# A long convolution by two short Fourier steps: an inverse of 64x64 cosine and sine sums instead of 64x128 complex ones

## The chip, the cores and the metric

The kernel runs on one core of a Trainium2 chip. The metric is the device time of one execution in microseconds; several executions are timed and their median is given. One execution is also recorded by the hardware profiler.

## The reference, cut to what matters

Two results for 2048 positions of 512 channels are mixed by a gate that depends on the position:

```python
x = A_u                                              # (1, 2048, 512)
g = sigmoid((x * gate_w).sum(-1, keepdims=True))
# a: a convolution along the 2048 positions
P = exp((dt * A)[:, :, None] * l)                    # 512 x 128 x 2048
K = einsum("dn,dnl,dn->dl", C, P, dt * B).real       # 512 filters of 2048 taps
y = irfft(rfft(pad(u)) * rfft(pad(K)))[:2048]        # transforms over 4096
a = y + u * Dskip
# b: a dense part
b = gelu(x @ w1 + b1) @ w2 + b2                      # 512 -> 1792 -> 512
return g * a + (1 - g) * b
```

All of it is in float32.

## The kernel before, in words

The program has two stages. The **front** (up to about 427 us) computes the 512 filters, the dense part b and a first short Fourier step of signal and filters; its order on every engine is written out by a planner that gives each piece a cost and a due time. The planner and the front are the same in both kernels. The front leaves in DRAM two arrays, tu_d for the signal and tk_d for the filters, of 32 frequencies with 128 rows of 512 channels each (64 points, real and imaginary). It also leaves the dense part's share of the output, already multiplied by 1 - g, in the output array itself.

The second stage, `conv`, has a hand-written order. Its loop runs over s = 0 to 15, two frequencies n = 2s and 2s + 1 at a time, and everything in it is 512 channels wide:

- `fetch` (L1056, L1059) brings a frequency's filter rows into a tile tk, of which there are eight, and for every fourth frequency a tile cc of matrices; L1179 brings the signal rows that did not fit before the loop. All of these are issued by SP.
- `taps` (bank p2k) and `signal` (bank p2u) are the second Fourier step: per s four matmuls each, with 128 rows and 64 output columns, the two frequencies of s side by side (L1084). ACT copies p2k to k (L1092).
- `product` multiplies signal and filter as complex numbers on DVE: six operations (L1106 to L1111) that give v, real and imaginary, two frequencies on top of each other in 64 rows each.
- `inverse` (bank pa, L1123) takes a frequency's 64 points back: for each of the two frequencies two matmuls of 64 rows by 128 columns, one with the real part of v and the matrix from cc, one with the imaginary part and a matrix g that `matrices` builds from cc on ACT (L1070, L1071). The 128 columns are 64 points, real and imaginary in turn.
- `turn` copies pa into one of six slots sa (ACT, L1129) and stores it to t4_d in DRAM (SP, L1131, shown as t_d). After each eighth frequency the group is read back with rows and frequencies exchanged into t3 (L1138, shown as t): four loads of 512 KB, issued by POOL for the first three groups and by ACT for the last.
- From s = 6 to 13, `dense` (L1148) loads the dense part's output rows back, 512 KB at a time, on SP.

On PE the order within one s is: signal of s + 1, taps of s + 2, inverse of s. On SP it is: the loads for three s later, then the stores of s, then dense's load. SP issues in order, and the program gives its transfers eight semaphores in turn, so each waits for the landing of the one eight before.

After the loop PE does what is left of the dense part (`rest`, L1159 to L1161) and four matmuls whose result nobody reads (`warm`, L1197). Then follows the last stage, eight rounds m of 2 x 128 output rows: in each, eight matmuls of 64 rows by 32 columns combine the 32 frequencies (bank pb, L1208), and the result is multiplied by g and added to the dense part, on DVE alone (L1219) or on ACT and POOL (L1216, L1217). SP stores each round (L1223); the last round leaves in two stores, on SP and ACT (L1221).

Of the kernel before, what the change touches and what calls it, by code (L numbers as in the profile page):

```python
# [9 lines left out]
F32 = mybir.dt.float32  # L10
# [7 lines left out]
P = 128  # L18
L = 2048
D = 512  # L20
# [53 lines left out]
N_US = N_ATTIC + N_LOFT  # L74
W_DVE = ((1, 0), (3, 0), (5, 0))

GROUP = 8

ASIDE = (1, 3, 6, 8, 11, 13)
PI = float(np.pi)  # L80
TWO_PI = 2.0 * PI
TURN = 2.0**32
# [12 lines left out]
def k0_order():  # L95
    return [8 * (n % 4) + n // 4 for n in range(32)]


def seat(n):

    return 4 * (n % 8) + n // 8


def constants():
# [10 lines left out]
    qn = np.arange(64)  # L115
# [6 lines left out]
    rows = np.zeros((2, 64, 32))  # L122
    for n, k in enumerate(k0_order()):
        rows[:, seat(n)] = er.T[k] / L
        rows[:, seat(n) + 32] = ei.T[k] / L
    g1 = rows.reshape(P, 32)

    ko = k0_order()  # L130
    f2 = np.zeros((32, 2, 64, 64))
    g2 = np.zeros((32, 64, 64, 2))
    for n, k in enumerate(ko):
        er, ei = om(4 * (q[:, None] * k + 32 * np.outer(q, k1)) + q[:, None])
        f2[n, 0], f2[n, 1] = er, -ei
        er, ei = om(4 * (qn[None] * k + 32 * np.outer(k1, qn)) + qn[None])
        g2[n, :, :, 0], g2[n, :, :, 1] = er, -ei
    f2 = f2.reshape(8, 4, P, 64).transpose(0, 2, 1, 3).reshape(8, P, 256)
    g2 = g2.reshape(8, 2, P, P).transpose(0, 2, 1, 3).reshape(8, P, 256)
# [111 lines left out]
def gated_mix(  # L251
# [18 lines left out]
    nc = tc.nc  # L270
# [5 lines left out]
    t4_d = dr.tile([4, 2, 2, GROUP, 32, D], F32, name="t4_d")  # L276
# [766 lines left out]
    def conv(pool, ps, late, attic, loft):  # L1043
# [3 lines left out]
        zs = [pool.tile([P, D], F32, name=f"z{k}", bufs=1) for k in range(2)]  # L1047
        us = places(attic, loft)
        ko = k0_order()
        c4s, mats, t2s = {}, {}, {}  # L1050

        def fetch(n):
            if n % 4 == 0:
                m = n // 4
                cc = pool.tile([P, 2, 256], F32, tag="cc", name=f"cc{m}", bufs=4)
                nc.sync.dma_start(cc, c2[m].rearrange("p (a b) -> p a b", a=2))  # L1056
                c4s[m] = cc
            t2s[n] = pool.tile([P, D], F32, tag="tk", name=f"tk{n}", bufs=N_TK)
            nc.sync.dma_start(t2s[n], tk_d[ko[n]])  # L1059

        def matrices(m):

            cc = c4s[m]
            f = cc[:, 0].rearrange("p (n k) -> p n k", n=4)
# [5 lines left out]
            nc.scalar.mul(g1[:, :, :, 0], g[:, :, :, 1], -1.0)  # L1070
# [43 lines left out]
        def inverse(s):  # L1114

            v = prod.pop(s)
            for i in range(2):
                pas[2 * s + i] = ps.tile([P, D], F32, tag="pa", name=f"pa{s}{i}", bufs=2)
            for c in range(2):
                w = mats[s // 2][1][c][:, s % 2]  # L1120
                for i in range(2):
                    r = slice(64 * i, 64 * i + 64)
                    nc.tensor.matmul(pas[2 * s + i], w[r], v[c][r], start=(c == 0), stop=(c == 1))  # L1123

        def turn(s):

            for n in (2 * s, 2 * s + 1):
                sa = sas[n % 6]
                nc.scalar.copy(sa, pas.pop(n))  # L1129
                g, k = divmod(n, GROUP)  # L1130
                nc.sync.dma_start(t4_d[g, :, :, k].rearrange("i c q d -> q (i c) d"), sa)  # L1131
                if k < GROUP - 1:
                    continue
                rows = t4_d[g].rearrange("i c k q d -> (i c k) q d")

                for h in range(0, 32, 8):
                    on = nc.gpsimd if n < 31 else nc.scalar
                    on.dma_start(t3[g:P:4, h : h + 8], rows[:, h : h + 8])  # L1138
# [25 lines left out]
        for n in range(N_TK):  # L1164
            fetch(n)
            if n == 1:
                t3 = pool.tile([P, 32, D], F32, name="t3", bufs=1)
                g1t = pool.tile([P, 32], F32, name="g1t", bufs=1)
        nc.sync.dma_start(g1t, g1)
        matrices(0)  # L1170
        taps(0)
        signal(0)
# [21 lines left out]

        warm = ps.tile([P, D], F32, tag="pa", name="warm", bufs=2)
        for _ in range(N_KEEP):
            nc.tensor.matmul(warm[0:64], mats[7][0][1][:, 3], zs[0], start=True, stop=True)  # L1197
        for s in range(N_LATE):
            z = mos[7][:, s]
            nc.vector.scalar_tensor_tensor(z, accs[s], gate[:, 1, 14 + s : 15 + s], z, ALU.mult, ALU.add)  # L1200

        for m in range(8):
            tag, n = ("pa", 2) if m % 3 == 2 else ("pu", 4)
            pbs = [ps.tile([P, D], F32, tag=tag, name=f"pb{m}{i}", bufs=n) for i in range(2)]
            for b in range(4):
                for i in range(2):
                    r = slice(64 * i, 64 * i + 64)
                    nc.tensor.matmul(  # L1208
                        pbs[i][32 * b : 32 * b + 32], g1t[r], t3[r, 4 * m + b], start=True, stop=True
                    )  # L1210
            for i in range(2):
                t = 2 * m + i
                z, g = mos[m][:, i], gate[:, 0, t : t + 1]
                if t in ASIDE:
                    a = sas[ASIDE.index(t)]
                    nc.scalar.mul(a, pbs[i], g)  # L1216
                    nc.gpsimd.tensor_add(z, z, a)  # L1217
                else:
                    nc.vector.scalar_tensor_tensor(z, pbs[i], g, z, ALU.mult, ALU.add)  # L1219
                if m == 7:  # L1220
                    (nc.sync, nc.scalar)[i].dma_start(out[t], z)  # L1221
            if m < 7:
                nc.sync.dma_start(out[2 * m : 2 * m + 2].rearrange("s p d -> p s d"), mos[m])  # L1223
# [22 lines left out]
def layout(inputs):  # L1246
# [4 lines left out]

    xl = xpq[:, qs].reshape(32, 16, 4, D).transpose(1, 2, 0, 3).reshape(16, P, D)

    xs = xpq.reshape(32, 8, 4, 2, D).transpose(1, 3, 2, 0, 4).reshape(16, P, D)
# [47 lines left out]
```

## Time and profile before

| | us |
|---|---|
| median of 3 runs | 552.06 |
| lowest, highest | 548.29, 552.96 |
| the profiled execution | 547.97 |
| its span, first to last instruction | 546.1 |
| loop over s, first inverse to last | 436.5 to 517.9 |
| last stage, first pb to the end of the span | 529.2 to 546.1 |

The profile names engines (PE for matmuls, PEld for their weight loads, DVE, ACT, POOL, SP) and writes each group as line, engine, operation, output<-input. A q behind an engine's name is its queue, the part that issues transfers and waits. A float32 matmul of the kernel shows as two instructions. Busy times of matmuls that run side by side overlap, so the distance from start to start tells more than the time of one. The share of DMA is the mean over the core's 16 DMA engines; it can pass 1 a little, as packets that share an engine are counted one by one.

### The profile page before, as it was taken

To read this page: it belongs to the slowest core of one execution; us is meant where nothing else is said; L and a number is where in the kernel's file an instruction comes from. 1 tells how busy PE (TensorE), PEld (TensorE's weight loads), DVE (VectorE), ACT (ScalarE), POOL (GpSimd) and SP (SyncE) were. 2 spreads that over 40 slices of the span, in tenths; PEclk is the share of its full clock that TensorE was granted. 3 is DMA by queue.
4 is the path that set the end of the run, shared out by engine and by line. 5 is a ranking of instruction groups with operands and counts; after the bars stand their busy time and mean duration, and the time that the engine had idled before them with its cause. 6 is when DMAs were issued, how large, how long until landed. Compare 5 with 4: busy or idle time off the path is not lost.

```text
span 546.1 us, 12354 instructions
## 1 busy us (share of the span) xinstructions
PE 523.0 (96%) x4882; PEld 393.9 (72%) x4882; DVE 426.8 (78%) x806; ACT 371.4 (68%) x630; POOL 41.3 (8%) x79
## 2 busy tenths in 40 slices
PE   7869999999999999999999999999999899999993
PEld 6637788998898879787988889889889533333450
DVE  6798999999999949979998899999311567676523
ACT  4989847799956599968659986496263554555312
POOL 2000000000000000000101010110011001010104
PEclk9869999999999999999999999999999999999998
DMA  8998583153683352564984227525539979999958
GB/s 264 335 298 291 199 262 106 69 166 112 144 266 134 116 158 78 184 230 98 215 271 96 79 39 176 96 80 117 156 42 190 315 259 294 370 368 402 338 216 308
DMA packets 82469, 108.35 MB, mean 198 GB/s; under 512 B 39446, under 2 KB 42522, under 8 KB 81900
## 3 DMA queue, kind: packets, MB, share of 16 engines
q1 hardware_dynamic: 77020, 86.56, 49.6%
q0 software_dynamic: 5056, 18.65, 13.2%
q10 hardware_dynamic: 336, 2.36, 1.2%
q8 instruction: 38, 0.62, 0.5%
q14 instruction: 19, 0.16, 0.1%
HBM read 61.93 MB, written 45.62 MB: 197 GB/s over the span
## 4 chain that ended last, share of the span: by engine, by line
PE 72%; DMA 11%; issue 5%; ACT 5%; SPq 2%; DVE 2%; POOL 1%; POOLq 0%; ACTq 0%; DVEq 0%
PE pk L653 10%; PE acc L917 8%; PE acc L919 8%; PE ph L869 8%; PE acc L918 7%; PE ph L870 7%; PE ph L871 7%; PE p2u L1084 5%; PE p2k L1084 5%; PE pa L1123 4%; DMA tu_d<-attic 2%; PE ph L378 2%; DMA attic<-in_xs_dram 2%; SPq L693 1%; ACT sk L678 1%
## 5 line engine op out<-in xcount | busy, mean ns | idle before, releaser
L869 PE MATMUL ph<-xh,wh 128*128 128x256 f32 x448 | 129.1, 288 | 4.0 <-ACT attic L396 2.2
L871 PE MATMUL ph<-xh,wl 128*128 128x256 f32 x448 | 128.0, 286 | 0.5 <-DVE wl L752 0.4
L870 PE MATMUL ph<-xlo,wh 128*128 128x256 f32 x448 | 127.7, 285 | 0.0
L869 PEld LDWEIGHTS ph<-xh,wh 128*128 128x128 f32 x448 | 86.2, 192 | 13.9 <-issue 4.8
L870 PEld LDWEIGHTS ph<-xlo,wh 128*128 128x128 f32 x448 | 86.3, 193 | 1.9
L917 PE MATMUL acc<-wh,hh 128*128 128x512 f32 x210 | 85.3, 406 | 2.1 <-ACT hh L889 1.9
L871 PEld LDWEIGHTS ph<-xh,wl 128*128 128x128 f32 x448 | 86.3, 193 | 1.1 <-DVE wl L752 1.1
L919 PE MATMUL acc<-wh,hl 128*128 128x512 f32 x210 | 83.4, 397 | 0.2 <-DVE hl L899 0.2
L918 PE MATMUL acc<-wl,hh 128*128 128x512 f32 x210 | 83.0, 395 | 0.0
L886 ACT ACTIVATE ph<-ph,b1t 128x256 f32<-128x256 f32 x112 | 50.4, 450 | 40.5 <-PE ph L871 38.5
L899 DVE TENSOR_TENSOR hl<-ph,hh 128x512 fp32r<-128x512 f32 (+1 forms) x62 | 38.3, 618 | 34.8 <-ACT hh L889 34.7
L653 PE MATMUL pk<-y,xc 128*32 128x64 f32 x2048 | 61.4, 290 | 0.0
L653 PEld LDWEIGHTS pk<-y,xc 128*32 128x32 f32 x2048 | 57.2, 136 | 3.7 <-issue 1.4
L917 PEld LDWEIGHTS acc<-wh,hh 128*128 128x128 f32 x210 | 39.8, 190 | 17.9 <-issue 7.6
L919 PEld LDWEIGHTS acc<-wh,hl 128*128 128x128 f32 x210 | 39.8, 190 | 11.5 <-DVE hl L899 2.8
L615 DVE TENSOR_TENSOR y<-y,ea 128x64 f32<-128x64 f32 (+4 forms) x80 | 45.3, 566 | 0.2
L918 PEld LDWEIGHTS acc<-wl,hh 128*128 128x128 f32 x210 | 39.7, 189 | 6.7
L460 DVE TENSOR_TENSOR loft<-xc,zz 128x256 f32<-128x256 f32 (+2 forms) x48 | 37.2, 776 | 2.4 <-ACT xc L586 2.0
L889 ACT CAST hh<-ph 128x512 fp32r<-128x512 f32 (+1 forms) x62 | 33.0, 533 | 7.5 <-PE acc L918 4.1
L461 DVE TENSOR_TENSOR loft<-xc,zz 128x256 f32<-128x256 f32 (+2 forms) x48 | 37.2, 774 | 0.0
L628 DVE TENSOR_TENSOR y<-y,loft 128x2048 f32<-128x2048 f32 x16 | 36.5, 2284 | 0.0
L1092 ACT COPY k<-p2k 128x512 f32<-128x512 f32 x32 | 18.7, 585 | 22.2 <-issue 12.2
(172 smaller groups left out, 923.3 us busy)
## 6 DMA issues: line engine op xcount, KB each, us to landing
tu_d<-attic SPq DMA_DIRECT2D x64, 128.0 KB, 3.6
tk_d<-sk SPq DMA_DIRECT2D x32, 256.0 KB, 4.5
tk<-tk_d SPq DMA_DIRECT2D x32, 256.0 KB, 5.1
t_d<-sa SPq DMA_DIRECT2D x32, 256.0 KB, 5.2
t<-t_d POOLq DMA_DIRECT2D x12, 512.0 KB, 7.5
attic<-tu_d SPq DMA_DIRECT2D x22, 256.0 KB, 4.3
attic<-in_xt_dram SPq DMA_DIRECT2D x16, 256.0 KB, 4.1
xh_d<-xh SPq DMA_DIRECT2D x8, 512.0 KB, 3.9
```

What stands on the lines that cost most here:

```text
L460: vec(2 * m, lambda: vv.tensor_mul(t, a, br), due, [ka, *kb], [kt])
L615: nc.vector.tensor_mul(both(n, 64 - 3 * n, n), both(0, 64 - n, n), an)
L653: nc.tensor.matmul(pks[q][32 * j : 32 * j + 32, gg], x[:, r, :, ch], y[:, r, :, ch], start=(r == 0), stop=(r == 1), skip_group_check=True,)
L869: nc.tensor.matmul(p, h, xh[xk][:, d], start=(d == 0), stop=False)
L870: nc.tensor.matmul(p, h, xlo[xk][:, d], start=False, stop=False)
L871: nc.tensor.matmul(p, lo, xh[xk][:, d], start=False, stop=(d == 3))
L886: nc.scalar.activation(phs[q][:, n], phs[q][:, n], AF.Gelu_apprx_tanh, bias=b1t[:, f : f + 1])
L899: nc.vector.tensor_sub(lo, phs[q][:, 0:nf], hi.bitcast(F32))
L917: nc.tensor.matmul(a, h, wh[1][w], start=start, stop=False)
L918: nc.tensor.matmul(a, h, wl[1][w], start=False, stop=False)
L919: nc.tensor.matmul(a, l, wh[1][w], start=False, stop=(j == 3))
L1084: nc.tensor.matmul(out[64 * i : 64 * i + 64], w, x, start=True, stop=True)
```

## The change

The inverse is taken about the middle of its 64 points. Instead of complex rows, each frequency's inverse gives sums with cosines and with sines at 32 distances from the middle: two matrices of 64 rows by 32 columns, side by side in 64 columns, real and the same for the real and the imaginary part of v. The two parts are written to the upper and lower 64 rows of pa. So a frequency has two matmuls of 64 rows by 64 columns, and the four of an s use four different quarters of the array.

The second matrix g and its two ACT operations per four frequencies go; cc has 384 columns instead of 512. A frequency's rows leave for DRAM in two stores of 64 rows, one for each part, 64 stores instead of 32. The rows of t3 then hold, for each frequency, cosine and sine sums of both parts, and the last stage takes all 128 rows in one matmul with 64 columns: four matmuls for a round instead of eight. Output rows come in another order, which the host's layout undoes; the rows of x for the dense part and the gate are laid out in the same order. warm uses another matrix of the same size. Sizes of arrays in DRAM, slots and banks stay.

```diff
-                cc = pool.tile([P, 2, 256], F32, tag="cc", name=f"cc{m}", bufs=4)
-                nc.sync.dma_start(cc, c2[m].rearrange("p (a b) -> p a b", a=2))
+                cc = pool.tile([P, 384], F32, tag="cc", name=f"cc{m}", bufs=4)
+                nc.sync.dma_start(cc, c2[m])
...
-            g = cc[:, 1].rearrange("p (s q c) -> p s q c", s=2, c=2)
-            g1 = pool.tile([P, 2, 64, 2], F32, tag="g1", name=f"g1{m}", bufs=2)
             nc.scalar.mul(f1[0:64], f[64:128], -1.0)
             nc.scalar.copy(f1[64:128], f[0:64])
-            nc.scalar.mul(g1[:, :, :, 0], g[:, :, :, 1], -1.0)
-            nc.scalar.copy(g1[:, :, :, 1], g[:, :, :, 0])
-            mats[m] = (f, f1), [z.rearrange("p s q c -> p s (q c)") for z in (g, g1)]
+            mats[m] = (f, f1), cc[:, 256:384].rearrange("p (s k) -> p s k", s=2)
...
             for i in range(2):
-                pas[2 * s + i] = ps.tile([P, D], F32, tag="pa", name=f"pa{s}{i}", bufs=2)
-            for c in range(2):
-                w = mats[s // 2][1][c][:, s % 2]
-                for i in range(2):
-                    r = slice(64 * i, 64 * i + 64)
-                    nc.tensor.matmul(pas[2 * s + i], w[r], v[c][r], start=(c == 0), stop=(c == 1))
+                n = 2 * s + i
+                pas[n] = ps.tile([P, D], F32, tag="pa", name=f"pa{s}{i}", bufs=2)
+                r = slice(64 * i, 64 * i + 64)
+                w = mats[n // 4][1][r, s % 2]
+                for c in range(2):
+                    nc.tensor.matmul(pas[n][64 * c : 64 * c + 64], w, v[c][r], start=True, stop=True)
...
-                nc.sync.dma_start(t4_d[g, :, :, k].rearrange("i c q d -> q (i c) d"), sa)
+                for c in range(2):
+                    nc.sync.dma_start(t4_d[g, c, :, k].rearrange("e q d -> q e d"), sa[64 * c : 64 * c + 64])
...
-                rows = t4_d[g].rearrange("i c k q d -> (i c k) q d")
+                rows = t4_d[g].rearrange("c e k q d -> (c e k) q d")
...
-            for b in range(4):
-                for i in range(2):
-                    r = slice(64 * i, 64 * i + 64)
+            for i in range(2):
+                for b in range(2):
+                    j = 4 * m + 2 * i + b
                     nc.tensor.matmul(
-                        pbs[i][32 * b : 32 * b + 32], g1t[r], t3[r, 4 * m + b], start=True, stop=True
+                        pbs[i][64 * b : 64 * b + 64], g1t[:, min(j, 1)], t3[:, j], start=True, stop=True
                     )
```

More of the change, by code (lines that the diff above doesn't have):

```diff
@@ L75 @@
 W_DVE = ((1, 0), (3, 0), (5, 0))
+ASIDE = (1, 3, 6, 8, 11, 13)
 GROUP = 8
[L79 removed]
 PI = float(np.pi)
@@ L101, in seat, with row_order @@
     return 4 * (n % 8) + n // 8
+def row_order():
+    p, rows = np.arange(32), []
+    for m in range(32):
+        rows.append(64 * p + (m - 1 if m else 63))
+        rows.append(64 * p + (63 - m if m else 31))
+    return np.concatenate(rows)
 def constants():
@@ L1167, in conv @@
                 t3 = pool.tile([P, 32, D], F32, name="t3", bufs=1)
-                g1t = pool.tile([P, 32], F32, name="g1t", bufs=1)
-        nc.sync.dma_start(g1t, g1)
+                g1t = pool.tile([P, 2, 64], F32, name="g1t", bufs=1)
+        nc.sync.dma_start(g1t, g1.rearrange("p (b k) -> p b k", b=2))
         matrices(0)
@@ L1196, in conv @@
         for _ in range(N_KEEP):
-            nc.tensor.matmul(warm[0:64], mats[7][0][1][:, 3], zs[0], start=True, stop=True)
+            nc.tensor.matmul(warm[0:64], mats[7][1][:, 1], zs[0], start=True, stop=True)
         for s in range(N_LATE):
```

48 lines of the change are left out of this document (32 added, 16 removed).

## The prediction

> **What bounds the kernel now.** I read the page first, then the chain of waits, then busy time by stretches, then the groups of instructions, the DMA issues and the clock. The page:
> ```profile
> span 546.1 us, 12354 instructions
> PE 523.0 (96%) x4882; PEld 393.9 (72%) x4882; DVE 426.8 (78%) x806; ACT 371.4 (68%) x630; POOL 41.3 (8%) x79
> ```
> PE is busy nearly all the time. The profiled execution took 547.97 us, 1.9 us beyond its span; the median of the three runs is 552.06 (548.29 to 552.96), so I work in this execution and scale by 552.06 / 547.97 = 1.0075 at the end. "Same" is within 1%, 5.5 us, about what a measurement of this kernel can tell from no change.
>
> Up to 427 us the two programs issue the same instructions; all that changes lies in the last 119 us, the convolution's second half. In its loop over s the chain of waits is PE alone, piece by piece (start, us, what):
> ```profile
> 484.34 1.72 PE p2k L1084 x8
> 486.06 1.92 PE pa L1123 x8
> 487.98 1.87 PE p2u L1084 x8
> ```
> One s takes 1.72 + 1.92 + 1.87 = 5.51 us, sixteen times, with no gap. But PE is not alone at its limit. Stretches of the loop (length, busy time by engine, PE clock, DMA share, GB/s):
> ```profile
> 436.48:438.46 1.98, 1.98 (x11) 0.75 (x12) 1.63 (x3) 0.58 (x1) 0.00 (x0) 1.00 0.39 145
> 438.46:453.00 14.54, 14.54 (x67) 4.51 (x66) 9.78 (x17) 7.48 (x15) 0.00 (x0) 1.00 0.78 256
> 453.00:469.50 16.50, 16.50 (x76) 5.24 (x74) 11.05 (x19) 9.41 (x20) 2.11 (x4) 1.00 0.99 342
> 469.50:486.00 16.50, 16.50 (x76) 5.24 (x74) 11.05 (x19) 8.07 (x16) 0.00 (x0) 1.00 1.02 354
> 486.00:501.73 15.73, 15.73 (x72) 5.23 (x72) 10.28 (x18) 8.82 (x19) 2.04 (x4) 1.00 1.02 403
> 501.73:522.04 20.31, 20.31 (x87) 9.38 (x84) 10.18 (x17) 6.64 (x12) 2.04 (x4) 1.00 0.91 336
> ```
> From 453 on the DMA engines are full as well. Share times length, summed over the six rows, is 79.8 us of 85.6: only 5.8 us of slack behind PE. DVE uses 11.05 of 16.5 us and ACT 9.41, so neither is near.
>
> **The change, part by part.** The groups that it touches or leans on:
> ```profile
> L1084 PE MATMUL p2k<-tk,cc 128*64 128x512 f32 x64 | 18.3, 593 | 1.6 <-DMA tk<-tk_d 1.6
> L1123 PE MATMUL pa<-v,cc 64*128 64x512 f32 x64 | 18.1, 641 | 0.0
> L1129 ACT COPY sa<-pa 128x512 f32<-128x512 f32 x32 | 17.2, 589 | 23.3 <-PE pa L1123 17.4 <-issue 5.9
> L1208 PE MATMUL pb<-t,g1t 64*32 64x512 f32 x128 | 7.6, 593 | 1.1 <-DVE attic L1219 1.1
> L1219 DVE SCALAR_TENSOR_TENSOR attic<-pb,gate,attic 128x512 f32<-128x512 f32 x6 | 4.4, 748 | 1.6 <-PE pb L1208 1.3
> L1217 POOL TENSOR_TENSOR attic<-attic,sa 128x512 f32<-128x512 f32 x4 | 5.0, 1275 | 1.1 <-ACT sa L1216 1.1
> L1070 ACT ACTIVATE g<-cc 128x128 f32<-128x128 f32 x8 | 2.6, 325 | 0.2
> ```
> *Inverse.* Four matmuls stay four, but 64 columns wide instead of 128. A matmul shows as two instructions. p2k's four (128 rows, 64 columns, two side by side) take 1.72 us, so one matmul alone is 0.86. The inverse now runs two row halves side by side: 2 x 0.86 plus 0.20 of start = 1.92. With 64x64 tiles all four can run at once: 0.86 + 0.20 = 1.06, a gain of 0.86 per s, 13.8 us in all. That this works is shown by the last stage's 64x32 tiles, eight at once:
> ```profile
> 525.58 3.65 PE L1197 MATMUL warm<-z,f 128*64 128x512 f32 x8
> 529.16 3.93 PE L1208 MATMUL pb<-t,g1t 64*32 64x512 f32 x64
> ```
> 64 instructions are 32 matmuls, four rounds of eight: 3.93 / 4 = 0.98 us each. The bounds are 0 (the tiles keep to pairs) and 13.8; I take 13.8, as rows and columns already run together there. The sixteen g copies that leave ACT (325 ns each) give nothing, since ACT waits anyway.
>
> *Stores.* Each of 32 frequencies leaves in two 64-row transfers instead of one of 128 rows. The old store, the front's 64-row store (issue ns min/median/max), and how long the old store took to land:
> ```profile
> L1131 SPq DMA_DIRECT2D t_d<-sa x32: 517/532/1633, 439.1 to 519.2; - x32
> L399 SPq DMA_DIRECT2D tu_d<-attic x64: 445/588/3489, 27.9 to 269.4; - x64
> DMA to landing us min/median/max: 2.6/5.2/9.9
> ```
> Half the size costs as much to issue: 4 x 0.45 to 0.59 instead of 2 x 0.53, so 0.7 to 1.3 us more per s on SP. Behind them in SP's queue stand the loads of tk for three s later, which PE needs. SP has room for this today:
> ```profile
> SPq L1131 <- ACT sa L1129: 30.6, 13, 5.1
> SPq L1059 <- DMA cc<-in_c_dram: 4.6, 2, 4.4
> ```
> It waits 30.6 us in these stores for ACT's copies; sixteen times 1.3 is 21. The second row shows the other limit: a tk load waited up to 4.4 us for the landing of a cc load issued eight transfers before. SP's transfers take eight semaphores in turn, so two half stores use up two places. I count this inside the DMA term. The change adds a wait too: ACT's copy into an sa slot waits for two landings, of the frequency six before. Behind it on ACT stand k's copies, which free p2k's banks for PE. The slot comes round after three s, 3 x 4.65 = 14 us, less about 2.5 for copy and issue; the slowest landing was 9.9, so this costs nothing unless transfers get slower still.
>
> *DMA.* This is the next thing late. The bytes hardly fall (cc loses 64 KB in each of five loads, 0.33 MB). Rate times length over the six rows gives 28.7 MB, without cc 28.4; of it 28.1 after 438.3, when the stores begin. At the 403 GB/s of the third full row that takes 69.7 us, at the 354 of the second 79.4. Which one a still fuller loop gets I cannot see, so I take 380: 74.0. With 2 us of idle early (5.8 now, less as PE runs faster) and 1.5 for the last landing, the last store lands at 438.3 + 74.0 + 3.5 = 515.8; the ends are 511.5 and 521.2. Now the half stores themselves. Two stretches of the front, the first with 64-row stores nearly alone, the second with a backlog of six of them between loads:
> ```profile
> 264.60:266.60 2.00, 2.00 (x18) 1.96 (x17) 2.00 (x4) 0.53 (x2) 0.00 (x0) 1.00 0.90 214
> 236.00:237.50 1.50, 1.50 (x10) 1.36 (x11) 0.41 (x2) 0.37 (x1) 0.12 (x1) 1.00 1.00 359
> ```
> Alone they get 214 / 0.90 = 238 GB/s, in a backlog 359. The 8.4 MB of stores cost 35.3 us at the one and 23.4 at the other: between 0 and 12 us more. The loop has a backlog, so I take 1.5. Last store: 517.3, against 522.04 now.
>
> The Trainium skill (SBUF — State Buffer, Door 1: the DMA port swizzle) says that partitions 0 to 63 reach only 8 of the 16 DMA ports, so that such a transfer gets about half the rate. The stretch at 238 GB/s agrees with it, the one at 359 does not; by the rule the whole 12 us would be due.
>
> *From the last store to the last stage.* When the last tk load, the last two stores and the first t load of the last group were issued, how long a transfer then took to land (us, last column), and when PE needed that tk:
> ```profile
> 494.04 0.32 SPq L1059 DMA_DIRECT2D tk<-tk_d  x1
> 518.64 1.16 SPq L1131 DMA_DIRECT2D t_d<-sa  x2
> 522.14 0.52 ACTq L1138 DMA_DIRECT2D t<-t_d  x1
> tk<-tk_d SPq DMA_DIRECT2D x1, 256.0 KB, 7.7
> t_d<-sa SPq DMA_DIRECT2D x1, 256.0 KB, 2.8
> t<-t_d ACTq DMA_DIRECT2D x1, 512.0 KB, 4.1
> 506.18 1.03 PE L1084 MATMUL p2k<-tk,cc 128*64 128x512 f32 x4
> ```
> Today t is there at 526.3, but PE reaches pb only at 529.16, after the rest of the dense part and warm: PE decides, by 2.9 us. After the change t arrives at 517.3 + 0.1 + 4.1 = 521.5. PE by itself would reach pb at 529.16 - 13.8 = 515.4. The last tk (landed 494.04 + 7.7 = 501.7) may hold it up: PE wants it 13 x 0.86 us sooner than 506.18, at 495.0, and the 21.2 MB before it need 55.8 us at 380 GB/s, which with 2 us of idle is 496.1, later with the half stores; call it 2 us, 517.5. So DMA decides, and pb starts at 521.5, 7.7 us earlier.
>
> *Last stage.* Four matmuls of 128 rows by 64 columns replace eight of 64 by 32 in each of eight rounds. That is p2k's shape: 1.72 us instead of 0.98, 13.8 in all. PE becomes the bound there, where evictions (748 ns on DVE; ACT and 1275 on POOL) and stores were. The end now:
> ```profile
> 535.48:540.98 5.50, 2.37 (x48) 0.63 (x32) 3.59 (x5) 1.95 (x3) 3.73 (x3) 1.00 1.02 379
> 540.36 0.86 SPq L1221 DMA_DIRECT2D out_dram<-attic  x1
> ```
> Today the stores queue at 379 GB/s, and pb to the end is 546.12 - 529.16 = 17.0 us. Afterwards 0.52 MB comes every 1.72 us, 305 GB/s, so only the last 0.79 MB waits: 13.9 + 0.9 for the last eviction, 0.4 to issue (the tk load's 0.32 and a little), 2.1 to move, and 2.0 for start and receipt (today 5.8 us pass from that row's start to the end; I put 3.4 of it down to some 1.3 MB queued ahead, 0.4 to the issue): 19.3, between 18.5 and 20.8 (today's 5.8 us kept nearly whole).
>
> *Clock.* PE would now idle some 4 us before pb. What idling does is seen early:
> ```profile
> 28.00:30.00 2.00, 0.54 (x2) 0.19 (x2) 2.00 (x9) 1.97 (x3) 0.00 (x0) 1.00 0.96 231
> 37.00:39.00 2.00, 2.00 (x12) 2.00 (x11) 2.00 (x3) 0.59 (x1) 0.00 (x0) 0.50 1.01 333
> ```
> After a thin stretch the granted clock was 0.50, and still was with PE fully busy again. Half speed for 3 us of pb costs 1.5; the bounds are 0 and 3.
>
> The Trainium skill (TensorE: Matmul & The Clock Gate, Part 1) puts the halving after one idle window of about 3.4 us. Of 4 us idle that is just within reach, and by it an estimate of 1.7 us would be lost.
>
> *Sum.* 521.5 + 19.3 + 1.5 = 542.3 against 546.1: 3.8 us less. 547.97 - 3.8 = 544.2, times 1.0075 = 548.2 us.
>
> **The rivals.**
> *PE stays the bound (0.26).* The full loop moves 403 GB/s, half stores cost nothing, PE never waits. For it: the third full row, and stores and loads that overlap. Against it: 342 and 354 in the rows where tk and tu loads are thickest. The last store lands at 511.5, pb starts at 515.7, no idle before it: 535.0, 11.1 us less, 540.9 us.
> *Half stores at the slow rate (0.24).* The sixteen DMA engines crowd on half the ports, c by c, in the loop too. For it: 238 GB/s above. Against: 359 in a backlog. 10.5 us more than I counted puts pb at 532.0 and the end at 552.8: 6.7 us more, 558.8 us. It ends slower than today once the last store lands after 521.1, that is from 3.8 us more than forecast.
> *The inverse still runs in pairs (0.07).* Nothing forbids it but pb's rows. Then pb starts as today, plus 0.6 for the issue of two more stores, and the last stage is longer: 529.8 + 19.3 = 549.1, 3.0 us more, 555.1 us.
>
> **How the numbers follow.** The forecast has 0.43, and its own range is 543 to 554, from 403 and 354 GB/s with the stores' bounds. Below 546.5 (1% faster) lie the first rival and a third of the forecast's range: 0.26 + 0.15 = 0.41. Above 557.6 lie six tenths of the second rival and the far tail of the others: 0.14 + 0.06 = 0.20. The rest, 0.39, is within 1%. The range 540 to 560 leaves out 0.1 at each side, the best of the first rival and the worst of the second.
>
> **What would show it.** Right: pa's eight instructions within about 1.1 us; gaps on PE before p2k that end with a tk load; DMA share near 1.0 from about 450 to 515; pb's groups spaced 1.72 us, after an idle PE that waited for t. Wrong: pa at 1.9 us; a loop of 4.65 us per s without gaps (first rival); GB/s below 330 at full share while t_d stores run (second). A longer queue on SP with idle DMA engines would mean that issuing, not moving, is the bound, which I did not price.

## The result, and the profile after

The changed kernel takes 558.36 us (median of 4 runs, 557.57 to 560.03), the kernel before beside it on the same chip 550.56 us (548.29 to 552.96). The ratio is 1.0154, with a 95% interval of 1.0123 to 1.0185: the change makes the kernel slower, where a small gain was forecast. The profiled execution took 560.03 us. Of its page, the span and the engines:

```profile
span 558.3 us, 12252 instructions
PE 525.1 (94%) x4818; PEld 392.6 (70%) x4818; DVE 426.8 (76%) x806; ACT 367.1 (66%) x614; POOL 41.4 (7%) x79
```

PE's share has fallen from 96% to 94%: it waits now. Its timeline early in the loop (start, us, what) shows that the inverse itself does what was forecast:

```profile
443.85 1.09 PE L1140 MATMUL pa<-v,cc 64*64 64x512 f32 x8
448.45 1.09 PE L1140 MATMUL pa<-v,cc 64*64 64x512 f32 x8
```

From the first start to the last end the four matmuls take 1.09 us instead of 1.98 (436.48 to 438.46 before), and one s comes 4.60 us after the other instead of 5.51. That does not last. Stretches of the loop (length, PE, PEld, DVE, ACT, POOL, PE clock, DMA share, GB/s), and the group of PE's with the longest waits (busy, mean ns, idle time ahead of it and what ended it):

```profile
455.00:470.00 15.00, 15.00 (x80) 4.21 (x78) 11.97 (x20) 8.64 (x17) 2.10 (x4) 1.00 0.97 330
470.00:485.00 15.00, 13.39 (x68) 4.04 (x66) 10.13 (x17) 6.99 (x14) 0.00 (x0) 1.00 0.94 306
485.00:500.00 15.00, 12.04 (x56) 3.13 (x50) 9.76 (x16) 5.96 (x12) 2.04 (x4) 1.00 0.98 342
500.00:515.00 15.00, 11.73 (x46) 3.56 (x48) 4.98 (x9) 5.21 (x10) 1.07 (x3) 0.77 0.97 326
```
```profile
L1101 PE MATMUL p2k<-tk,cc 128*64 128x512 f32 x56 | 18.4, 632 | 7.8 <-DMA tk<-tk_d 7.8
```

From 470 us on PE has gaps, 7.8 us in all, and they end with tk loads. The surprise stands in the last two columns. The kernel before moved 342 to 403 GB/s in full stretches at a share of 0.99 to 1.02. Now that PE asks for data faster, the DMA engines move less, 306 to 342, and are less busy as well (0.94 to 0.98). What SP, which issues those transfers, waits for in the loop (us in total, times, longest):

```profile
SPq L1149 <- DMA attic<-out_dram: 6.0, 2, 5.5
SPq L1149 <- ACT sa L1146: 5.5, 3, 4.2
SPq L1149 <- DMA t_d<-sa: 5.0, 3, 2.3
SPq L1149 <- DMA cc<-in_c_dram: 2.9, 1, 2.9
```

Before, SP waited 30.6 us in its stores for ACT's copies, which means that it was ahead. Now that is 5.5 us, and in the same line (L1149) it waits 13.9 us for the landing of transfers that it issued itself, eight before. Added up over all of SP's instructions, from the first inverse to the last store's issue: issuing takes 58.2 us instead of 42.1, waiting for landings 21.1 instead of 11.8, and waiting for ACT 8.3 instead of 31.9. So the lead that SP had is used up by both, more by issuing than by landings. The chain of waits shows how both reach the end (start, us, what):

```profile
492.90 10.23 DMA tk<-tk_d
...
503.27 4.17 PE p2k L1101 x8
507.44 1.92 PE pa L1140 x8
...
513.68 11.77 DMA attic<-out_dram
...
528.65 2.36 DMA t_d<-sa
...
531.11 4.21 DMA t<-t_d
535.32 0.14 issue
535.46 8.80 PE pb L1226 x32
...
545.09 7.11 PE pb L1226 x32
```

A tk load takes 10.23 us. Then a load of the dense part takes 11.77 us, and the stores of the last three frequencies stand behind its landing in SP's queue; the last one is issued at 528.65, 9.4 us later than before. There are two more losses on PE: p2k takes 4.17 us instead of 1.72, and the first half of pb 8.80 instead of 7.11. The clock's column at both places:

```profile
503.00:505.00 2.00, 1.73 (x4) 1.04 (x6) 0.00 (x0) 0.32 (x1) 0.00 (x0) 0.50 1.02 338
537.00:539.00 2.00, 2.00 (x8) 0.85 (x6) 0.33 (x1) 0.69 (x1) 0.05 (x1) 0.50 0.55 234
```

PE had been idle 4.92 us ahead of the first and 4.02 us ahead of the second. Summed up, the span is 12.1 us longer: 2.8 before the first inverse, in a part that is the same program in both and varies from run to run (the first inverse stands between 435.5 and 441.4 us in the profiled executions of this document); +6.2 from the first inverse to the landing of the last store (91.8 instead of 85.6, where 80.8 was forecast); -2.7 from there to pb; +5.8 from pb to the end (22.8 instead of 17.0).

### The profile page after: what moved, and what is told of

The parts are those of the page before. It is cut to its first block, busy times and chain, and to the rows that moved or that the text cites. A ratio compares the mean times of both kernels' runs of the same rounds, so it can differ in the third digit from the quotient of the medians.

```text
span 558.3 us, 12252 instructions
## 1 busy us (share of the span) xinstructions
PE 525.1 (94%) x4818; PEld 392.6 (70%) x4818; DVE 426.8 (76%) x806; ACT 367.1 (66%) x614; POOL 41.4 (7%) x79
## 4 chain that ended last, share of the span: by engine, by line
PE 74%; DMA 15%; ACT 4%; SPq 3%; DVE 2%; issue 1%; ACTq 0%
PE pk L676 9%; PE acc L940 9%; PE ph L892 8%; PE acc L942 8%; PE acc L941 8%; PE ph L893 8%; PE ph L894 8%; DMA tk<-tk_d 7%; PE p2k L1101 4%; PE p2u L1101 3%; PE pb L1226 3%; PE ph L401 2%; DMA attic<-out_dram 2%; PE pa L1140 2%; ACT sk L701 1%; SPq L716 1%
## 5 line engine op out<-in xcount | busy, mean ns | idle before, releaser
L941 PEld LDWEIGHTS acc<-wl,hh 128*128 128x128 f32 x210 | 39.8, 190 | 6.7
L1109 ACT COPY k<-p2k 128x512 f32<-128x512 f32 x32 | 18.7, 585 | 32.0 <-issue 20.7
```

Source lines behind the costliest of these rows:

```text
L941: nc.tensor.matmul(a, h, wl[1][w], start=False, stop=False)
```

## The experiments

Three theories: *stores*, the two half stores per frequency are what lengthens the loop; *traffic*, the transfers bound it whatever their size; *end*, the loss is the longer last stage with its halved clock. Every ratio is to the kernel before, timed beside it, with its 95% interval. "Loop" is from the first inverse to the landing of the last store in the one profiled execution; GB/s and DMA share are those of the stretch from 470 to 485 us. A profiled execution can stand some us off its kernel's median (e2_split_alone's took 557.2 us, its median is 552.63), so the ratios decide.

| kernel | ratio | loop, us | share, GB/s |
|---|---|---|---|
| before | 1 | 85.6 | 1.01, 355 |
| the change | 1.0154 [1.0123, 1.0185] | 91.8 | 0.94, 306 |
| e5_inverse_alone | 0.9843 [0.9805, 0.9880] | 78.2 | 1.03, 381 |
| e1_one_store | 0.9893 [0.9857, 0.9929] | 78.5 | 1.03, 378 |
| e2_split_alone | 1.0059 [1.0028, 1.0089] | 94.7 | 0.90, 312 |
| e4_old_last | 1.0054 [1.0025, 1.0082] | 93.5 | 0.91, 297 |
| e3_halves | 1.0104 [1.0068, 1.0140] | 88.3 | 0.96, 319 |
| e3_mixed | 1.0135 [1.0092, 1.0178] | 90.0 | 0.96, 320 |
| e8_tiny | 1.0050 [1.0028, 1.0073] | 85.6 | 0.93, 316 |
| e18_tiny_pool | 0.9956 [0.9930, 0.9982] | 80.0 | 1.05, 390 |
| e9_pool | 0.9994 [0.9970, 1.0018] | 82.3 | 1.03, 382 |
| e15_act | 1.0125 [1.0081, 1.0169] | 89.5 | 0.96, 324 |
| e16_halves_pairs | 1.0114 [1.0076, 1.0153] | 86.6 | 0.91, 304 |
| e17_halves_tk10 | 1.0034 [1.0014, 1.0054] | 85.6 | 0.95, 347 |
| e7_keep | 1.0106 [1.0061, 1.0150] | 92.1 | 0.93, 312 |
| e10_pairs | 0.9915 [0.9887, 0.9944] | 81.1 | 1.03, 383 |
| e12_dense_pool | 0.9908 [0.9873, 0.9943] | 78.7 | 1.03, 375 |
| e13_tk10 | 0.9850 [0.9819, 0.9881] | 76.2 | 1.05, 394 |

### Which part of the change

**e1_one_store.** The new inverse's columns are put in the order sums-first, t4_d gets a layout in which the 128 rows of sa follow each other, and g1's rows follow that:

```diff
-    t4_d = dr.tile([4, 2, 2, GROUP, 32, D], F32, name="t4_d")
+    t4_d = dr.tile([4, GROUP, P, D], F32, name="t4_d")
...
-                for c in range(2):
-                    nc.sync.dma_start(t4_d[g, c, :, k].rearrange("e q d -> q e d"), sa[64 * c : 64 * c + 64])
+                nc.sync.dma_start(t4_d[g, k], sa)
...
-                rows = t4_d[g].rearrange("c e k q d -> (c e k) q d")
+                rows = t4_d[g].rearrange("k (a q) d -> (k a) q d", a=4)
```

> The changed kernel, but a frequency leaves in one store of 128 rows, into a DRAM layout in which those rows follow each other; inverse and last stage as changed. Three theories. Stores: the two half stores per frequency are what lengthens the loop (first inverse to the last store's landing 91.8 us after the change, 85.6 before); then the loop falls to about 80 us, as the forecast had it without its 1.5 us for half stores, pb starts some 8 us earlier than before the change, and the time is 0.98 to 0.99 of the kernel before. Traffic: the transfers of the loop bound it whatever their size; then the loop stays at 85 us or more and the time is 1.005 to 1.015. End: the loop is as long as before and the longer last stage with its halved clock (pb to the end 22.8 us instead of 17.0) is the whole loss; then 1.010 to 1.015.

Measured: 0.9893, inside the stores theory's range, outside the other two. The stretches and the end of its chain of waits:

```profile
455.00:470.00 15.00, 15.00 (x82) 4.01 (x80) 12.24 (x21) 9.12 (x18) 2.12 (x4) 1.00 1.02 364
470.00:485.00 15.00, 15.00 (x82) 4.29 (x80) 11.40 (x19) 8.54 (x16) 0.00 (x0) 1.00 1.03 378
485.00:500.00 15.00, 13.22 (x68) 3.55 (x64) 11.05 (x18) 7.39 (x15) 2.04 (x4) 1.00 1.04 410
500.00:515.00 15.00, 15.00 (x78) 7.08 (x75) 7.36 (x12) 5.47 (x10) 2.04 (x4) 1.00 1.03 392
```
```profile
512.32 7.63 DMA t_d<-sa
...
520.05 3.88 DMA t<-t_d
523.92 0.14 issue
524.06 7.10 PE pb L1225 x32
```

With the same bytes the engines now move 364 to 410 GB/s at a share above 1, and pb starts at 524.06 instead of 535.46, at full clock. The step from 0.9893 to 1.0154 is 0.0261 of 549 us, or 14.3 us. The half stores and their stepped layout in DRAM are both in it; e3_halves, below, has half stores in the flat layout, and the step to it is 0.0211, or 11.6 us.

The whole loop in one row, for the changed kernel and for e1_one_store:

```profile
439.24:531.01 91.77, 83.93 (x395) 28.48 (x394) 54.41 (x89) 37.99 (x71) 6.18 (x12) 0.96 0.93 308
```
```profile
441.44:519.95 78.51, 76.73 (x390) 26.00 (x390) 54.48 (x89) 37.91 (x71) 6.20 (x12) 1.00 0.97 360
```

Rate times length is 28.3 MB in both. Share times length is about 85 us in the first and 76 in the second. So of the 13.3 us between the loops only 4 to 5 are time in which, by this count, the DMA engines had nothing to do. In the other 8 to 9 they were busy but moved less for it, and no run here shows why.

**e5_inverse_alone** is the kernel before with the four 64x64 matmuls:

```diff
-            for c in range(2):
-                w = mats[s // 2][1][c][:, s % 2]
-                for i in range(2):
-                    r = slice(64 * i, 64 * i + 64)
-                    nc.tensor.matmul(pas[2 * s + i], w[r], v[c][r], start=(c == 0), stop=(c == 1))
+            for i in range(2):
+                r = slice(64 * i, 64 * i + 64)
+                for c in range(2):
+                    w = mats[s // 2][1][c][r, s % 2, 0:64]
+                    nc.tensor.matmul(pas[2 * s + i][64 * c : 64 * c + 64], w, v[c][r], start=True, stop=True)
```

> The kernel before, with only the inverse made of four 64 by 64 tiles at once (it takes 64 of the 128 columns of each matrix and leaves out the sum over the two parts, so the output differs); one store per frequency and the old last stage. Stores theory: the faster inverse shortens the loop by the forecast's 4 to 8 us, ratio 0.985 to 0.993. Traffic theory: the loop is full of transfers anyway, PE waits for tk as long as it gains, ratio 0.997 to 1.003. End theory says nothing here beyond a gain of 0 to 4 us.

Measured: 0.9843, 8.6 us faster. So the traffic theory falls: there is room for a faster PE. SP's wait for ACT's copies in its stores, 30.6 us before, is smaller here, though the stores are the old ones:

```profile
SPq L1131 <- ACT sa L1129: 17.1, 13, 4.1
```

The faster inverse alone takes some 13 us of SP's lead away.

**e2_split_alone** cuts the old store in two:

```diff
-                nc.sync.dma_start(t4_d[g, :, :, k].rearrange("i c q d -> q (i c) d"), sa)
+                for j in range(2):
+                    nc.sync.dma_start(
+                        t4_d[g, :, :, k, 16 * j : 16 * j + 16].rearrange("i c q d -> q (i c) d"),
+                        sa[64 * j : 64 * j + 64],
+                    )
```

> The kernel before, with only its store cut into two of 64 rows (partitions 0 to 63 and 64 to 127). Stores theory: the 32 more transfers cost at least the 5.8 us of slack that the DMA engines had behind PE, PE gets gaps before p2k, ratio 1.005 to 1.015. Traffic and end theories: the half stores are hidden under PE's 5.51 us per s, ratio 0.998 to 1.003, and t arrives later by less than the 2.9 us that PE had in hand.

Measured: 1.0059, inside the stores theory's range. With PE's 5.51 us per s the half stores cost 3 us, where they cost 11.6 to 14.3 with the faster inverse.

**e4_old_last** gives the changed kernel the old shape of the last stage:

```diff
...
-                        pbs[i][64 * b : 64 * b + 64], g1t[:, min(j, 1)], t3[:, j], start=True, stop=True
+                        pbs[i][32 * b : 32 * b + 32], g1t[r, 0, 0:32], t3[r, 4 * m + b], start=True, stop=True
```

> The changed kernel with the last stage's matmuls in their old shape (eight of 64 rows by 32 columns per round, on the new tiles; so the last stage computes something else than the reference). End theory: pb to the end falls from 22.8 to 17 or 18 us and the ratio to the kernel before from 1.015 to about 1.004. Stores or traffic theory: the stage is only 2 to 3 us shorter, ratio 1.010.

Measured: 1.0054, close to what the end theory said: with the half stores in place the longer last stage and its clock cost 0.0100, 5.5 us. With one store they cost much less, 0.0050 (e1 against e5, some 2.7 us, with intervals that overlap). So the end adds to the loss but is not its root: the kernel with the long last stage and one store is faster than the kernel before.

### What it is about the half stores

**e3_halves** and **e3_mixed** start from e1_one_store, with its store cut again, once by halves of the partitions and once by even and odd ones:

```diff
-                nc.sync.dma_start(t4_d[g, k], sa)
+                for c in range(2):
+                    nc.sync.dma_start(t4_d[g, k, 64 * c : 64 * c + 64], sa[64 * c : 64 * c + 64])   # e3_halves
+                    nc.sync.dma_start(t4_d[g, k, c:P:2], sa[c:P:2])                                  # e3_mixed
```

> The one-store kernel (0.9893 of the kernel before), with its store cut again into two of 64 rows, partitions 0 to 63 and 64 to 127, each flat in DRAM. Ports (rows of one half move slower, c by c) and places (two half stores use two of the eight transfers that may be under way on SP's queue, and two issues): as slow as the changed kernel, ratio 1.010 to 1.018. Address pattern (the changed kernel's stores step through DRAM by 16-row strides and take 0.51 to 0.60 us to issue, the flat ones 0.32): then these flat halves are as fast as the one store, ratio 0.988 to 0.993.

> As the kernel with flat half stores, but one store takes the even partitions and the other the odd ones: as many transfers of the same size, each spread over all partitions. Ports: fast again, ratio 0.988 to 0.994, t_d stores moving at the rate of the loads. Places: as slow as the flat halves, 1.010 to 1.018. If both have a share it falls between.

Measured: 1.0104 and 1.0135, both slow, with intervals that overlap. Rows spread over all partitions help nothing, so it is not the side of the partitions that slows the half stores; by the Trainium skill (SBUF — State Buffer, Door 1: the DMA port swizzle) the even and odd rows would have had the full rate, and here they did not. The address pattern could not be told apart as meant, since issuing did not become cheaper. The store's instructions in e1_one_store and e3_halves (issue ns, min/median/max):

```profile
L1148 SPq DMA_DIRECT2D t_d<-sa x32: 319/320/984, 443.2 to 512.3; - x32
```
```profile
L1149 SPq DMA_DIRECT2D t_d<-sa x64: 445/551/1082, 438.6 to 522.6; - x64
```

Half as many rows take longer to issue, 0.55 us against 0.32. So three candidates are left: the places in SP's queue (eight transfers may be under way, and each one holds a place until it lands), SP's issue time, and work for each transfer on the DMA engines.

**e8_tiny** and **e18_tiny_pool** add to e1_one_store a transfer of one row, 2 KB, behind every store, on SP's queue and on POOL's:

```diff
                 nc.sync.dma_start(t4_d[g, k], sa)
+                nc.sync.dma_start(bin_d[n : n + 1], sa[0:1])       # e8_tiny
+                nc.gpsimd.dma_start(bin_d[n : n + 1], sa[0:1])     # e18_tiny_pool
```

> The one-store kernel (0.9893), plus, behind every store, a second one of a single row (2 KB, into a scratch tensor): as many transfers on SP's queue as with half stores, but the same bytes within 0.06 MB and only one of the 16 DMA engines per extra transfer. Places theory (a transfer issued waits for the landing of the one eight before, and eight transfers of which a third are small hold too few bytes under way to fill the DMA engines): as slow as the half stores, ratio 1.005 to 1.015, DMA share below 1.0 and gaps on PE for tk. Overhead theory (each transfer costs time on every DMA engine that it uses): 0.989 to 0.992.

> The one-store kernel plus a 2-KB transfer behind every store, as in the kernel that came to 1.005, but issued on POOL's queue. The DMA engines do the same extra work (the 2 KB are cut into 16 pieces, one for each engine, on either queue); SP's places and issue time are as with one store. Places or issue: 0.988 to 0.993. Overhead on the engines for each transfer: 1.002 to 1.008.

Measured: 1.0050 on SP and 0.9956 on POOL. 64 KB of bytes in 32 transfers on SP cost three quarters of what the half stores cost there (0.0157 of 0.0211). Their own packets are not it. The packets of the loop in e8_tiny (436 to 523 us) and e18_tiny_pool (436 to 517 us):

```profile
DMA packets 12896, 28.63 MB, mean 329 GB/s; under 512 B 1476, under 2 KB 2116, under 8 KB 12507
```
```profile
DMA packets 13780, 28.49 MB, mean 352 GB/s; under 512 B 2463, under 2 KB 3103, under 8 KB 13390
```

On POOL the 2 KB are cut into many small packets, about a thousand more in all; on SP they stay whole, contrary to what the second expectation says of them. The kernel with more packets for the DMA engines is the faster one. So the queue matters: the DMA share is 1.05 from 470 to 485 us with the extra transfers on POOL and 0.93 with them on SP. What SP waits for in e8_tiny:

```profile
SPq L1149 <- ACT sa L1147: 7.5, 5, 3.7
SPq L1150 <- DMA t_d<-sa: 6.6, 4, 5.5
SPq L1167 <- DMA loft<-out_dram: 5.5, 2, 4.4
SPq L1083 <- DMA tk<-tk_d: 4.5, 5, 2.8
```

Most of it is again the landing of its own transfers, eight before. What POOL did not give back (0.9956 against 0.9893, intervals that all but touch) is 3.5 us, and 2.1 of it stand at the very end of the program (under e9_pool).

**e9_pool** moves the second half store of e3_halves to POOL:

```diff
-                    nc.sync.dma_start(t4_d[g, k, 64 * c : 64 * c + 64], sa[64 * c : 64 * c + 64])
+                    on = (nc.sync, nc.gpsimd)[c]
+                    on.dma_start(t4_d[g, k, 64 * c : 64 * c + 64], sa[64 * c : 64 * c + 64])
```

> The kernel with flat half stores (1.0104), with the second half of each frequency issued on POOL's queue, which counts its own eight transfers. Places theory: SP is back to as many transfers per s as with one store, ratio 0.988 to 0.996 (a little for half stores that stand behind POOL's t loads while these wait). Overhead theory: the transfers are as many and as small, so 1.008 to 1.014.

Measured: 0.9994, just above the places theory's range and far from the overhead theory's. The DMA engines are full again (1.03, 382 GB/s), and half of the loss is gone. This run and e8_tiny tell places from issue time. SP issues for 39.6 us in the loop of e8_tiny and for 39.8 in that of e9_pool, in 107 and 76 transfers. It waits for landings 29.6 us in the one and 16.7 in the other, and for ACT 8.6 and 22.0. At the same issue time it is the kernel with more transfers on SP's queue whose SP has lost its lead. So in e8_tiny it is places, as far as these two can be compared.

Of the 5.5 us between this kernel and e1_one_store (0.9994 against 0.9893) the profiled loops have 3.8 (82.3 against 78.5), and 2.1 stand behind pb (22.71 us to the end against 20.65). There POOL ends later than all others. Its last instructions, here and in e1_one_store (ns, min/median/max, first and last start in us):

```profile
L1315 POOLq DRAIN  x3: 51/93/7844, 537.2 to 545.5; - x3
```
```profile
L1313 POOLq DRAIN  x3: 51/93/5231, 538.1 to 544.4; - x3
```

The longest takes 7.84 us instead of 5.23 and ends at 545.0 us, 2.0 after SP is done with its last waits; in e18_tiny_pool it is much the same, 7.86. In the loop POOL's half stores stand behind its t loads, and ACT's copies wait 13.2 us for half stores to land and free a slot:

```profile
ACT sa L1146 <- DMA t_d<-sa: 13.2, 4, 5.7
```

**e15_act** puts that half store on ACT, in the same way (`nc.scalar` for `nc.gpsimd`).

> The kernel with flat half stores (1.0104; its half stores take 0.55 us each to issue, the one store 0.32), with the second half of each frequency issued by ACT. In the program's waits ACT's transfers share the same eight semaphores with SP's, so places are as scarce as before, while SP has 32 x 0.55 = 17.6 us less to issue. Issue theory (SP's time is what the half stores use up): 0.990 to 1.000. Places theory: 1.008 to 1.02, above it if ACT, which now waits for landings too, holds up the copies that free PE's banks.

Measured: 1.0125. Places are as scarce as before and the loss stays, but this does not clear issue time: SP no longer brings tk late, and ACT has become late in its place. The groups of PE with the longest waits:

```profile
L1101 PE MATMUL p2k<-tk,f 128*64 128x512 f32 x52 | 14.5, 638 | 7.3 <-ACT f L1090 7.3
L1140 PE MATMUL pa<-v,cc 64*64 64x512 f32 x128 | 21.2, 653 | 2.4 <-ACT sa L1146 2.4
```

**e16_halves_pairs** loads the two tk of an s in one transfer:

```diff
-            t2s[n] = pool.tile([P, D], F32, tag="tk", name=f"tk{n}", bufs=N_TK)
-            nc.sync.dma_start(t2s[n], tk_d[ko[n]])
+            if n % 2 == 0:
+                pair = pool.tile([P, 2, D], F32, tag="tk", name=f"tk{n}", bufs=N_TK // 2)
+                nc.sync.dma_start(pair, tk_d[ko[n] : ko[n] + 9 : 8].rearrange("a p d -> p a d"))
+                t2s[n], t2s[n + 1] = pair[:, 0], pair[:, 1]
```

> The kernel with flat half stores (1.0104), with the two tk loads of an s in one transfer of 512 KB, so seven transfers per s instead of eight and 219 KB in the mean instead of 192. With one store the same pairing gained nothing (0.9915 against 0.9893). Places theory: half of what half stores cost comes back, 0.998 to 1.004. Issue theory: 0.3 to 0.4 us of SP's time per s out of the 1.6 that the half stores add, 1.004 to 1.009. If neither count nor issue matters, 1.0104 within 0.003.

Measured: 1.0114, nothing back; both theories missed. SP has 98 transfers in its loop instead of 108, but it waits 23.0 us for landings, where it waited 21.3 in e3_halves: a pair takes 6.0 us in the median to land and a single tk 4.5, so it holds its place longer. So the number of transfers per s is not the whole of it. That the half stores and the loads of the dense part still stand ahead of the next tk would explain it, but was not tried.

**e17_halves_tk10** gives e3_halves ten tk buffers:

```diff
-N_ATTIC, N_LOFT, N_TK = 11, 8, 8
+N_ATTIC, N_LOFT, N_TK = 11, 8, 10
```

> The kernel with flat half stores (1.0104), with ten tk buffers instead of eight. If what half stores do is to keep tk's loads waiting in SP's queue (places or issue), a tk asked for one s sooner takes most of PE's gaps away: 0.990 to 1.000. If they make the DMA engines move less in all (share 0.95 to 0.96 instead of 1.02 to 1.04), the tk come sooner but the stores later, and it gains no more than the 2 us that the same step gained with one store (0.9893 to 0.985): 1.004 to 1.008.

Measured: 1.0034, a third of the loss, between the two ranges and nearer to the second. PE's 6.0 us before p2k are no longer put down to tk but to f, a matrix that ACT makes from cc:

```profile
L1101 PE MATMUL p2k<-tk,f 128*64 128x512 f32 x56 | 16.0, 629 | 6.0 <-ACT f L1090 6.0
```

The f in question comes late because of what stands ahead of it on ACT (start, us, what, idle time before it):

```profile
492.65 0.58 ACT L1146 COPY sa<-pa 128x512 f32<-128x512 f32 x1 [3.32 <-DMA t_d<-sa]
496.92 0.58 ACT L1146 COPY sa<-pa 128x512 f32<-128x512 f32 x1 [3.68 <-DMA t_d<-sa]
497.53 0.41 ACT L1089 ACTIVATE f<-cc 64x256 f32<-64x256 f32 x1
```

That is not for want of cc: the load was issued at 483.26 us, and SP had its place back for another transfer at 489.29. ACT waits for the half stores of three s earlier to land, so that a slot of sa is free; those took up to 10.3 us. With tk out of the way, the next to be late are the slots.

**e7_keep** is the changed kernel with eight warm matmuls instead of four ahead of the last stage:

```diff
-N_KEEP = 4
+N_KEEP = 8
```

> The changed kernel with 8 instead of 4 warm matmuls ahead of the last stage, so that PE has no 4.0 us gap before pb. If the halved clock at pb's start is what that gap costs, pb runs at 7.1 us per half from its start and pb to the end falls from 22.8 to about 21: ratio 1.012 instead of 1.0154. If the clock falls for another reason, no change: 1.0154 within 0.002.

Measured: 1.0106. The interval (1.0061 to 1.0150) just overlaps with that of the changed kernel, so the time alone does not decide; the trace does. The start of pb in its chain of waits:

```profile
529.45 3.71 DMA t<-t_d
533.16 0.14 issue
533.30 7.10 PE pb L1226 x32
```

PE is idle 1.75 us instead of 4.02, pb's first half takes 7.10 us instead of 8.80, and pb to the end is 21.1 us instead of 22.8: the halved clock at pb was the gap's doing.

### A version faster than both

e1_one_store beats both kernels already. Three edits on top of it: tk in pairs (**e10_pairs**, the edit of e16 above), the eight loads of the dense part on POOL's queue (**e12_dense_pool**, `nc.gpsimd` in `dense`), ten tk buffers (**e13_tk10**, the edit of e17).

> The one-store kernel, with the two tk loads of one s in one transfer of 512 KB. Places theory: five transfers per s instead of six hold more bytes under way; with one store the DMA engines are full already (share 1.02 to 1.04 from 455 us to 515 us), so it gains 0 to 3 us: 0.984 to 0.990. A loop that were still short of places would gain more than that; a tk that comes only as a pair could also come later, at most 0.993.

> The one-store kernel (0.9893), with the eight loads of the dense part issued on POOL's queue instead of SP's. Places theory: they leave eight places on SP that tk, tu and stores can use, tk arrives sooner in the second half of the loop and the gap of 1.8 us on PE goes: 0.984 to 0.989. As far as the DMA engines are full (share 1.02 to 1.04) it changes nothing: 0.987 to 0.992. A load that stands behind POOL's t loads, or that takes turns with SP's transfers there, could cost up to 3 us: 0.995.

> The one-store kernel, with ten tk buffers instead of eight (in the room that the smaller matrices have freed), so that tk is asked for one s sooner. The one-store loop has a DMA share of 0.85 from 440 to 455 us, and PE waits 1.8 us for tk near 497: with deeper prefetch some of these 2.2 us of idle engines are used, 0.984 to 0.989. If bytes alone set the end and the early idle has another cause (places), 0.987 to 0.992.

Measured: 0.9915, 0.9908 and 0.9850. The first two change nothing that can be told from e1's 0.9893. The third may: its interval (0.9819 to 0.9881) overlaps with e1's, and its trace shows both things that were expected of it. The second stretch below had a DMA share of 0.85 at its place in e1_one_store (440 to 455 us) and has 0.99 here, and PE does not wait:

```profile
440.00:455.00 15.00, 15.00 (x80) 4.20 (x78) 12.24 (x21) 8.37 (x16) 0.00 (x0) 1.00 0.99 332
485.00:500.00 15.00, 15.00 (x80) 4.06 (x76) 11.56 (x19) 8.34 (x16) 0.00 (x0) 1.00 1.04 407
```

At 541.65 us (540.06 to 543.36, beside 549.44 for the kernel before) it is the fastest kernel here that computes the whole.

## Why the prediction failed, point by point

*The inverse* was right: 1.09 us against a forecast 1.06, 0.91 us saved per s while nothing else is late (forecast 0.86), and worth 8.6 us by itself (e5).

*Stores* is the step that failed, at the words "I count this inside the DMA term". The step before it had the facts: twice as many issues, two of eight places for each frequency, tk behind them, a queue whose slack was SP's 30.6 us of waiting for ACT. But it gave them no term of their own. The DMA term then charged the half stores 1.5 us at a rate that the engines were taken to keep up, with 12 us as the bound. Measured: 11.6 us by the ratios with the layout kept flat (e1 to e3_halves), 14.3 with the stepped layout of the change; in the profiled loops 9.8 and 13.3.

The room that the step found in SP's queue was not there. It set 21 us of more issuing against 30.6 us of waiting for ACT. The issuing was about right: the stores take 39.4 us to issue instead of 19.3, 1.26 us more per s, at the top of the 0.7 to 1.3. But the 30.6 us belonged to the slow inverse; with the fast one and the old stores they are 17.1 (e5), less than the 21. And SP's waits for landings, which the step named but gave no time, grew by 9.3 us. With SP's lead went the full load of the DMA engines on which the term rested. The wait for slots of sa, which was to cost "nothing unless transfers get slower still", was 1.5 us in the changed kernel; in e17, where tk was not late, it was the next limit.

*DMA* without the half stores came out. The forecast had the loop at 515.8 - 436.5 = 79.3 us without them; e1_one_store measured 78.5. Its whole sum without the 1.5 us is (547.97 - 5.3) x 1.0075 = 546.7 us, 0.990 of the kernel before; measured, 0.9893. That it agrees so well is in part luck: the last stage was 1.4 us longer than forecast, and the 1.5 us charged for the clock were not lost with one store.

*Last store to last stage*: 4.45 us, forecast 4.2. *The last stage*: 20.7 us from pb to the end with one store, forecast 19.3; within its bounds of 18.5 to 20.8. The sum had PE's eight rounds without a stop; in the trace PE waits 0.8 us between the fourth and the fifth for an eviction on DVE.

*Clock*: 1.5 us were charged at pb, and 1.7 (8.80 - 7.10) were lost there. The forecast missed that late loads make such a gap in the middle of the loop as well: from 503 us p2k and the inverse lost (4.17 - 1.72) + (1.92 - 1.02) = 3.4 us. The Trainium skill (TensorE: Matmul & The Clock Gate, Part 1) puts the halving after one idle window of about 3.4 us; the trace agrees, gaps of 4.92 and 4.02 us halved the clock, and 1.75 us in e7_keep did not.

*The rival of half stores at the slow rate* had nearly the measured time, 558.8 against 558.36, by luck, with the wrong mechanism: rows on all partitions are as slow (e3_mixed). Its sign, less than 330 GB/s at full share, did show (306 at 0.94), but it shows in e3_mixed too (320 at 0.96), so it was no sign of the ports. Nearest to the right one was the last sentence of "What would show it", a longer queue on SP, as something not priced; but the engines were less busy, not idle, and it was not issuing alone.

What is shown: that the half stores carry the loss; that it is not the partitions they come from; that extra transfers on SP's queue leave the DMA engines less busy (0.93), while extra ones on POOL's leave them full (1.05); and, from e8_tiny beside e9_pool, that places can do this at the same issue time. What is not settled: how the loss of the half stores themselves divides between places and issue time, since neither e15 nor e16 took one away cleanly; and why the engines, in most of the time lost, were busy and yet moved less.

## What to carry to other kernels

Count transfers per pass of a loop, not only bytes: a queue in program order with a limited number under way has a capacity in transfers, and how far it runs ahead is its slack. Before a store is split, look at what the issuing engine waits for; if that is a producer it has room, and if the change makes the producer faster, the room shrinks (30.6 us to 17.1 here). Where an operand's layout forces a split, change the layout of the scratch in DRAM instead, so that one transfer takes all rows.

## What was not expected of the hardware

A store of 64 rows took longer to issue than one of 128 rows into the flat layout, 0.55 against 0.32 us in the median. A transfer of 2 KB, once per frequency, cost 8.6 us in the whole (0.0157 of 549) on SP's queue. And the DMA engines moved less for the time that they were busy when the extra transfers stood on SP's queue: from 470 to 485 us 319 GB/s at a share of 0.96 in e3_halves, which is 332 for a full share, against 378 at 1.03, which is 367, in e1_one_store; why the busy engines were slower is not settled here. POOL's closing DRAIN took 7.84 us in e9_pool, where POOL had issued 79 transfers in the whole program, and 5.23 in e1_one_store, where it had issued 47; 2.1 us of that are in the time from pb to the end.
